# Attention and a feed-forward layer on one core: three copies out of PSUM change engine, one row sum is partly pre-added, and 34 warm-up matmuls are added

## The chip, the cores and the metric

The kernel runs on one core of a Trainium2 chip. Its time is what the device takes for one execution, in microseconds (us). A core has five engines that run side by side and each work through their own instructions in order: TensorE (PE; its weight loads are listed apart as PEld), VectorE (DVE), ScalarE (ACT), GpSimd (POOL) and SyncE (SP, which here only issues DMA transfers). They wait for each other by semaphores. PSUM is the memory into which TensorE writes; VectorE and ScalarE read it, and the large memory beside it is SBUF.

## The reference

For 8 batches of 12 heads, 448 positions and 64 channels:

```python
q_n, k_n = (rmsnorm(q, g_q), rmsnorm(k, g_k))          # x / sqrt(mean(x*x) + 1e-6) * g
scores = scale * np.matmul(q_n, k_n.transpose(0, 1, 3, 2))
attn = softmax(scores)                                  # exp(scores - max) / sum
attn_out = np.matmul(attn, v)
x = attn_out.transpose(0, 2, 1, 3).reshape(3584, 768)
h = x @ w_in                                            # 768 x 2048
out = np.maximum(0.01 * h, h) @ w_out                   # 2048 x 768
```

All inputs and the output are float32.

## The kernel before

The work is cut into `NU` = 24 units. A unit is four heads of one batch, so that three units make a batch. The order of all instructions is written out by hand (`tc.manual_schedule`): what is emitted first on an engine runs first there.

**One unit.** `load` (SP) and `load_v` (POOL) bring q, k and v. `prep_sq` or `prep_sqp` squares (ScalarE or GpSimd), `prep_ssq` sums the squares (VectorE), `prep_rinv` makes the inverse root with Ln and Exp (ScalarE), `prep_norm` multiplies (VectorE), and the result is transposed, in the first units by TensorE (`prep_tr`, `tr`) and from unit 6 on by a DMA (`prep_trd`). `prep_g` then scales the queries with the two gains (VectorE). The scores of a unit come in seven tiles t = 0 to 6, each of 128 x 896 in two PSUM banks (`score`, line 199). `ex` (line 218) makes the exponentials `et` on ScalarE, one instruction per tile, with the bias `eb`. This bias, the negative of a maximum taken from tile 0, comes from `shift_max` and `shift_mm`: a reduce on VectorE (line 236), a small product `dg` (238), two small matmuls (248), a reduce (249) and a scaling (257).

**PSUM.** The score tiles take turns in two tiles of two banks each (`slot`, line 193). The product of the exponentials with v (PV) of the unit before takes one of the two in between (`pv_slot`). The other four banks are handed out by `aux`.

**The end of a unit.** From unit 4 to unit 22 (`narrow`), PV of unit u-1 runs behind the first scores of unit u. `zcol` sums the exponentials with matmuls against ones (line 307, four matmuls of 224 columns for each tile). `pv_out` copies PV from PSUM to SBUF (`x32`, line 319, one buffer), ScalarE takes Ln and Exp of the negative (`zcol_ln`, `zcol_inv`), four DMAs issued by SP spread the inverse sums over the partitions (`rz`, line 334), and `xmul_sb` (VectorE) or `xmul_pool` (GpSimd) multiplies the two (line 344). In units with an entry in `ADDED`, `add_e` first adds that many exponential tiles on VectorE (line 292), so that `zcol` needs fewer matmuls: with 4, it takes 3 tiles and the sum in place of 7 tiles.

**The order in a unit.** Each unit has four steps d = 0 to 3 with score tiles 0; 1 and 2; 3 and 4; 5 and 6. At the start of a unit the order is:

```python
qk(u, STEPS[d]); shift_max(u)
pv_slot(u - 1); zcol(u - 1); shift_mm(u); pv_out(u - 1)
ex(u); zcol_ln(u - 1)
```

Behind each step `fill` puts pieces of the feed-forward layer of earlier batches on TensorE (`moe1`, line 386; `moe2`, line 427; `seven`, line 468), by a fixed cost per piece, and between them small jobs for the other engines: the norms of unit u+2, the inverse sums, differences of weights (`weight_sum`, line 443). VectorE also evicts the results of `moe2` (line 431) and forms sums of activations for `seven` (lines 449 to 458).

**The start.** Units 0 to 2 run before there is any feed-forward work to fill in. There `warm(n, bank)` (line 766) issues n matmuls of 128 x 128 on constant ones; nothing reads their result. Before the change there are groups of 32 and 42 ahead of the first transposes, of 6 ahead of the first `shift_mm`, and of 12, 8, 10, 8 and 12 later, up to 29 us.

Of the kernel before, what the change touches and what calls it, by code (L numbers as in the profile page):

```python
# [18 lines left out]
def kernel(  # L19
# [11 lines left out]
    nc = tc.nc  # L31

    B, H, S, D = q.shape
# [78 lines left out]
    st = {}  # L112
# [25 lines left out]
    def buf(u, name):  # L138
        if name not in st[u]:
            shape, dtype, bufs = SHAPES[name]  # L140
            st[u][name] = prep_p.tile(shape, dtype, tag=name[:2] if bufs == 3 and name != "qkT" else name, bufs=bufs, name=name)
        return st[u][name]
# [3 lines left out]
    def prep_sq(u, c=ALL, tis=BOTH):  # L146
        for ti in tis:
            nc.scalar.activation(buf(u, f"sq{ti}")[:, :, c[0]:c[1]], raw[u][ti][:, :, c[0]:c[1]], AF.Square)  # L148
# [44 lines left out]
    def slot():  # L193
        return psum.tile([P, 2, 512], FP32, tag="sT", bufs=2, name="sT")

    def score(u, t, banks):
        for r in range(2):
            for a in range(2):
                nc.tensor.matmul(banks[a][64 * r:64 * r + 64, 0:S].rearrange("p (t x) -> p t x", t=NS),  # L199
                                 kT(u, r, a, t), qT(u, r, a), start=True, stop=True)  # L200

    def qk(u, steps):
        st[u]["sT"] = []
        for t in steps:
            sT = slot()
            score(u, t, (sT[:, 0], sT[:, 1]))
            st[u]["sT"].append((t, sT))

    def ex(u):
        s = st[u]  # L210
        if "et" not in s:
            s["et"] = epool.tile([P, NS, 2, S], FP16, tag="et", name="et")
        for t, sT in s["sT"]:
            if isinstance(sT, list):
                for a in range(2):
                    nc.scalar.activation(s["et"][:, t, a], sT[a][:, 0:S], AF.Exp, bias=s["eb"], scale=1.0)
            else:
                nc.scalar.activation(s["et"][:, t], sT[:, :, 0:S], AF.Exp, bias=s["eb"], scale=1.0)  # L218
# [62 lines left out]
                                     e[64 * r:64 * r + 64, a], start=(i == 0), stop=(i == len(ets) - 1))  # L281

    HS = S // 2
    ADDED = {u: 4 for u in (10, 11, 13, 16, 17, 19)}
    ADDED.update({3: 5, 4: 5, NU - 1: 5})
    ADDED.update({u: 3 for u in (8, 14, 20, 22)})

    def add_e(u):
        s = st[u]
        s["ea"] = zpool.tile([P, 2, S], FP16, tag="ea", name="ea")  # L290
        for t in range(1, ADDED[u]):
            nc.vector.tensor_tensor(s["ea"], s["et"][:, 0] if t == 1 else s["ea"], s["et"][:, t], op=ALU.add)  # L292

    def z_tiles(u):
        s = st[u]
        ets = [s["et"][:, t] for t in range(NS)]
        return ets[ADDED[u]:] + [s["ea"]] if "ea" in s else ets

# [17 lines left out]
    def pv_out(u):  # L316
        s = st[u]
        s["x32"] = zpool.tile([P, 2, S], FP32, tag="x32", name="x32")
        nc.scalar.copy(s["x32"], s["pslot"][:, :, 0:S])  # L319

    def zcol_ln(u):
        s = st[u]
# [13 lines left out]
    def xmul_sb(u):  # L336
        xmul_pool(u, nc.vector)
# [426 lines left out]
    def warm(n, bank):  # L764
        for x in range(n):
            nc.tensor.matmul(bank[:, P:2 * P], onesp, onesp, start=True, stop=True)

    with tc.manual_schedule():
# [7 lines left out]
        wbank = aux([P, 512], FP32, "warm")  # L776
# [1 line left out]
        for a in range(2):  # L778
            nc.vector.scalar_tensor_tensor(gdup[:, a], grow[:, 0], 0.125, grow[:, 1], op0=ALU.mult, op1=ALU.mult)
        nc.tensor.matmul(gps[:, 0:1], gdup.rearrange("o a d -> o (a d)"), one32, start=True, stop=True)  # L780
        warm(42, wbank)
        prep_sq(0, CA, (0,))
        prep_sq(0, CB, (0,))
        prep_sq(0, ALL, (1,))
# [11 lines left out]
        def tr(u, ti, chunks, tp=None):  # L796
            if tp is None:
                tp = aux([P, NS, P], FP16, "tp")
            for c, copy in chunks:
                for x in range(*c):  # L800
                    nc.tensor.transpose(tp[:, x, :], buf(u, "n16")[:, ti, x].rearrange("p a d -> p (a d)"), ident16)
                copy(buf(u, "qkT")[:, ti, c[0]:c[1]], tp[:, c[0]:c[1]], ti == 0)
            return tp

        tr(0, 0, ((CA, acopy),))
        tr(0, 0, ((CB, acopy),))
        tpk = tr(0, 1, ((K0, vcopy),))
        prep_sq(1, ALL, (0,))
        qk(0, STEPS[0])
        shift_max(0)  # L810
# [7 lines left out]
        load_v(1)  # L818
        load_v(2)
        shift_bank(0)  # L820
        warm(6, st[0]["pb"])
        shift_mm(0)
        prep_ssq(1)

# [56 lines left out]
        for f in range(2):  # L881
            load_w_out(8 * f, 8)
        qk(1, (2,))
        ex(1)
        trn(2, 0, vcopy)
        qk(1, (3,))
# [27 lines left out]
        prep_sqp(5)  # L914
        load_v(5)
        qk(2, (2,))
        ex(2)
        trn(3, 0, vcopy)
        trn(3, 1, vcopy)
# [31 lines left out]
        for u in range(3, NU):  # L951
            for d in range(4):
                if d > 0 or u > 3:
                    qk(u, STEPS[d])
                    if d == 0:
                        shift_max(u)
                        if u == 6:
                            xmul_sb(u - 2)
                        if narrow(u - 1):
                            pv_slot(u - 1)  # L960
                            zcol(u - 1)
                            shift_mm(u)
                            pv_out(u - 1)
                        else:
                            zsum_slot(u - 1)
                            pv(u - 1)
                            shift_mm(u)
                            zinv(u - 1)
                    ex(u)
                    if d == 0 and narrow(u - 1):  # L970
                        zcol_ln(u - 1)
                if d == 2 and ADDED.get(u, 0) > 3 and u < NU - 1:
                    add_e(u)
                    if u > 4:
                        xmul_sb(u - 1)
                jobs = []

                def job(fn, *args):
                    jobs.append(lambda: fn(*args))

                if d == 0:
                    if u == 3:
                        prep_norm(4)
                        gate(4)
                    elif narrow(u - 1):
                        if u < NU - 1:
                            job(zcol_inv, u - 1)
                    else:
                        xmul(u - 1)
                    if u + 4 < NU:  # L990
                        job(load, u + 4)
                    if u + 3 < NU:
                        load_v(u + 3)
                    if u < 6:
                        prep_sqp(u + 3)
                if d == 1 and narrow(u - 1) and not 5 <= u < 8 and ADDED.get(u, 0) < 4:
                    xmul_pool(u - 1)
                if u == NU - 1:
                    if d == 1:
                        job(zcol_inv, u - 1)  # L1000
                if fed(u, d) and u > 3:
                    push(u // NQ - 1)
                if (u, d) in ((3, 1), (4, 0)):
                    for ti in range(2):
                        prep_tr(u + 1, ti, VV)
                if d == 1 and 5 <= u < NU - 1:
                    job(prep_g, u + 1)
                if u + 2 < NU:
                    if d == 1:
                        if ADDED.get(u) == 3:  # L1010
                            job(lambda u: (prep_ssq(u + 2), add_e(u)), u)
                        else:
                            for ti in range(2):
                                job(prep_ssq, u + 2, ALL, (ti,))
                    if d == 2:
                        job(prep_rinv, u + 2)
                        for ti in range(2):
                            job(prep_norm, u + 2, ALL, (ti,))
                        if u > 3:
                            job(prep_trd, u + 2)  # L1020
                if d == 1 and 4 <= u < 8:
                    job(weight_sum, u - 4, 0)
                if d == 0 and 5 <= u < 9:
                    job(weight_sum, u - 5, 1)
                if d == 2 and 6 <= u < 8:
                    job(xmul_sb, u - 1)
                if d == 1 and u == NU - 2:
                    jobs.append(lambda: None)
                    job(add_e, u)
                if u == NU - 2 and d == 0:  # L1030
                    for n, tile_ in ((1, (raws, "rq", 3)), (2, (raws, "rk", 3)), (3, None), (4, (prep_p, "sq", 3))):
                        job(win_sum, n, 1, tile_)
                    for n in (3, 1, 2, 4):
                        job(x_sum, LATE, n)
                if u == NU - 1 and d == 3:
                    job(add_e, u)
                    job(xmul_sb, u - 1)
                if d == 3 and 6 <= u < NU - 3:
                    for ti in range(2):
                        job(prep_sq, u + 3, ALL, (ti,))  # L1040
                fill(u, d, jobs)
# [39 lines left out]
```

## Time and profile before

| | |
|---|---|
| time, median of 4 runs | 418.29 us (417.57 to 418.68) |
| the profiled execution, its own time | 418.64 us |
| its span, from first to last instruction | 416.9 us |
| TensorE busy in 0 to 44 us | 34.15 us |
| TensorE busy in 60 to 121 us | 60.16 us |
| copies of PV on ScalarE (line 319) | 19 of 906 ns |
| warm-up matmuls (line 766) | 130 |

All times inside the execution count from the start of its span. In a timeline row the columns are the start, the duration, the engine, the line of the kernel, the operation with its output and inputs, the shapes, and how many instructions are merged; brackets give the idle time of the engine just before and what ended it. In a row of groups the first figures behind the bar are busy time in all and the mean duration in nanoseconds of one. Matmuls are pipelined and the duration of one (352 ns for 448 columns) is longer than the distance to the next (about 190 ns), so a row of n matmuls is read by the start of the row behind it. Units 5, 6, 7 and 8 start at 69.3, 81.4, 95.5 and 111.2 us.

### The profile page before, as it was taken

The page shows a single profiled execution, that of the slowest core. Times are in us where ns is not written, and L with a number is a line of the kernel's source. Part 1 is how long each engine was busy: PE and PEld are TensorE (multiplying, and loading weights), DVE is VectorE, ACT ScalarE, POOL GpSimd, SP SyncE. Part 2 cuts the span into 40 slices and gives each one's busy share as a digit, 9 for nine tenths or more (in the row PEclk, how much of TensorE's full clock was granted, in tenths as well). Part 3 has the DMA queues.
Part 4 walks back from the last instruction along what each step waited for, and adds up shares of the span by engine and source line. Part 5 has one row for each costly group of instructions (what it writes and reads, how often), then busy time and mean ns, then how long its engine had stood idle before and what let it go on. Part 6 is the DMA issues. An engine that isn't in the chain of part 4 may idle for free.

```text
span 416.9 us, 9315 instructions
## 1 busy us (share of the span) xinstructions
PE 398.8 (96%) x3807; PEld 218.8 (52%) x3807; DVE 301.7 (72%) x485; ACT 303.6 (73%) x474; POOL 68.7 (16%) x70
## 2 busy tenths in 40 slices
PE   7777999999999999999999999999999999999995
PEld 7454444454445544455455544455445557559862
DVE  5888797887688756866668756767669788567762
ACT  5998888778887699867887689867985657644500
POOL 1868432200010200010020200020002202000000
PEclk9999999999999999999999999999999999999999
DMA  5999998889566995678664986688542470023022
GB/s 191 274 257 249 241 249 161 198 156 215 150 155 85 215 246 100 152 179 176 157 156 69 220 205 130 143 183 180 156 91 46 120 165 2 16 68 77 2 75 77
DMA packets 71951, 62.41 MB, mean 150 GB/s; under 512 B 36325, under 2 KB 67045, under 8 KB 71909
## 3 DMA queue, kind: packets, MB, share of 16 engines
q1 hardware_dynamic: 61312, 49.62, 47.5%
q0 software_dynamic: 10272, 11.80, 18.2%
q8 instruction: 30, 0.49, 0.5%
q10 hardware_dynamic: 324, 0.39, 0.3%
q14 instruction: 13, 0.10, 0.1%
HBM read 45.61 MB, written 11.01 MB: 136 GB/s over the span
## 4 chain that ended last, share of the span: by engine, by line
PE 78%; DVE 9%; ACT 8%; issue 2%; DMA 1%; SPq 0%; DVEq 0%; ACTq 0%
PE hps L386 27%; PE sT L199 8%; PE sT L364 5%; PE ma L468 5%; PE md L468 5%; ACT et L218 5%; PE mc L468 5%; PE bank L588 4%; PE bank L468 4%; PE op L427 4%; DVE n L171 3%; PE mb L468 2%; PE zc L307 2%; PE sT L468 2%; DVE sT L236 1%
## 5 line engine op out<-in xcount | busy, mean ns | idle before, releaser
L218 ACT ACTIVATE et<-sT,eb 128x896 f16<-128x896 f32 x166 | 159.5, 1010 | 18.7 <-PE sT L199 16.9
L386 PE MATMUL hps<-xt,win 128*128 128x448 f16 x600 | 120.8, 353 | 0.2 <-DVE xt L373 0.2
L386 PEld LDWEIGHTS <-win 128*128 128x128 f16 x612 | 56.8, 98 | 58.1 <-issue 9.7
L380 ACT ACTIVATE gt<-hps 128x448 f16<-128x448 f32 x100 | 54.0, 556 | 6.1 <-PE hps L386 5.3
L199 PE MATMUL sT<-qkT 64*64 64x448 f16 x664 | 52.4, 363 | 4.4 <-ACT et L218 3.6
L159 DVE TENSOR_REDUCE ssq<-sq 128x14 f32<-128x896 f32 (+2 forms) x49 | 50.1, 1057 | 0.8 <-ACT sq L148 0.7
L468 PEld LDWEIGHTS <-sa 128*128 128x128 f16 x352 | 32.8, 98 | 26.3 <-issue 6.1
L128 POOL DMA_DIRECT2D vt<-in_v_dram x24 | 17.9, 746 | 173.2 <-PE sT L364 166.5
L319 ACT COPY x<-sT 128x896 f32<-128x896 f32 x19 | 17.2, 906 | 34.0 <-DVE sT L249 34.0
L199 PEld LDWEIGHTS <-qkT 64*64 64x64 f16 x672 | 15.4, 104 | 37.8 <-issue 33.4
L468 PEld LDWEIGHTS <-gt 128*128 128x128 f16 x264 | 25.2, 98 | 18.9 <-issue 2.4
L171 DVE TENSOR_TENSOR n<-rq,rinv 128x896 f16<-128x896 f32 (+2 forms) x25 | 28.1, 1125 | 9.5 <-ACT rinv L165 9.5
L344 POOL TENSOR_TENSOR xt<-x,rz 128x896 f16<-128x896 f32 x9 | 19.0, 2114 | 79.3 <-DMA rz<-zs 72.0
L364 PE MATMUL sT<-et,vt 64*64 64x448 f16 x532 | 28.5, 349 | 0.3
L427 PE MATMUL op<-wout,gt 128*128 128x384 f16 x160 | 28.4, 326 | 0.0
L236 DVE TENSOR_REDUCE sT<-sT 128x1 f32<-128x896 f32 x22 | 24.1, 1093 | 4.7 <-PE sT L199 4.5
L292 DVE TENSOR_TENSOR ea<-ea,et 128x896 f16<-128x896 f16 x25 | 15.6, 625 | 15.6 <-ACT et L218 14.8
L364 PEld LDWEIGHTS <-vt 64*64 64x64 f16 x672 | 20.7, 107 | 11.3 <-issue 1.7
L171 DVE TENSOR_TENSOR n<-rk,rinv 128x896 f16<-128x896 f32 (+2 forms) x26 | 26.1, 1010 | 0.0
L427 PEld LDWEIGHTS <-gt 128*128 128x128 f16 x192 | 17.6, 98 | 14.3 <-issue 3.0
L468 PE MATMUL ma<-wout,gt 128*128 128x384 f16 x128 | 23.5, 326 | 0.0
L292 DVE TENSOR_TENSOR ea<-et 128x896 f16<-128x896 f16 x13 | 8.8, 677 | 11.9 <-ACT et L218 11.8
(143 smaller groups left out, 542.5 us busy)
## 6 DMA issues: line engine op xcount, KB each, us to landing
rq<-in_q_dram SPq DMA_DIRECT2D x24, 448.0 KB, 4.4
rk<-in_k_dram SPq DMA_DIRECT2D x24, 448.0 KB, 6.0
out_dram<-ost SPq DMA_DIRECT2D x52, 192.0 KB, 3.1
rz<-zs SPq DMA_DIRECT2D x76, 112.0 KB, 2.3
vt<-in_v_dram POOLq DMA_DIRECT2D x24, 224.0 KB, 5.6
win<-in_moe_w_in_dram POOLq DMA_DIRECT2D x8, 384.0 KB, 13.5
wout<-in_moe_w_out_dram POOLq DMA_DIRECT2D x2, 1536.0 KB, 28.1
out_dram<-ost SPq DMA_DIRECT2D x4, 96.0 KB, 2.1
```

Of the source, the lines that this page charges most:

```text
L159: nc.vector.tensor_reduce(buf(u, "ssq")[:, ti, :, c[0]:c[1]], buf(u, f"sq{ti}")[:, :, c[0]:c[1]], axis=AXL.X, op=ALU.add)
L171: nc.vector.tensor_tensor(buf(u, "n16")[:, ti, c[0]:c[1]].rearrange("p s a d -> p a s d"), src[:, :, c[0]:c[1]], buf(u, "rinv")[:, ti, :, ...
L199: nc.tensor.matmul(banks[a][64 * r:64 * r + 64, 0:S].rearrange("p (t x) -> p t x", t=NS), kT(u, r, a, t), qT(u, r, a), start=True, stop=True)
L218: nc.scalar.activation(s["et"][:, t], sT[:, :, 0:S], AF.Exp, bias=s["eb"], scale=1.0)
L236: nc.vector.tensor_reduce(s["spare"][:, 511:512], sT[:, :, 0:S], axis=AXL.XY, op=ALU.max)
L292: nc.vector.tensor_tensor(s["ea"], s["et"][:, 0] if t == 1 else s["ea"], s["et"][:, t], op=ALU.add)
L344: eng.tensor_tensor(xts[b][:, g], s["x32"], s["rz"], op=ALU.mult)
L364: nc.tensor.matmul(s["pv"][r][64 * a:64 * a + 64, 0:S], vts[u % NV][64 * r:64 * r + 64, a, t], s["et"][64 * r:64 * r + 64, t, a], start=(t ...
L380: nc.scalar.activation(dst, src, AF.Prelu, bias=0.0, scale=1.0, alpha=0.01)
L386: nc.tensor.matmul(hps[:, 0:S], win16[:, kt // 2, kt % 2, ts(ft, P)], xt[:, kt // 2, kt % 2], start=(kt == 0), stop=(kt == KT - 1))
L427: nc.tensor.matmul(op2[:, 0:HC], gt[:, ft, ds(col(t), P)], wout16[:, ft, ds(HC * half, HC)], start=(ft == 0), stop=(ft == FT - 1))
L468: nc.tensor.matmul(bank[:, 0:HC], a[:, f], b[:, f], start=(first and f == 0), stop=(f == HF - 1), skip_group_check=not first)
```

## The change

Four things change:

- `pv_out` of units 4, 5 and 6, which is emitted in units 5, 6 and 7, becomes a copy on VectorE. There it stands behind the bias of the next unit, which is the instruction emitted just before it. The other 16 copies stay on ScalarE.
- Unit 7 gets an entry of 4 in `ADDED`. So VectorE adds its tiles 0 to 3 in step 2 of unit 7, and `zcol` of unit 7 has 16 matmuls instead of 28.
- With this entry, `xmul_sb` of unit 6 follows directly on `add_e`, and the job that made it further behind in the same step is taken out.
- `warm` grows: 48 instead of 42 ahead of the first transposes, 10 instead of 6 ahead of the first `shift_mm`, and new groups of 6 ahead of the first scores of unit 0, of 6 behind tile 2 of unit 1 and of 12 behind tile 2 of unit 2, the last two each ahead of transposes.

On TensorE, VectorE and ScalarE nothing else changes place; the order on SP's and GpSimd's queues is the same.

```diff
-    ADDED = {u: 4 for u in (10, 11, 13, 16, 17, 19)}
+    ADDED = {u: 4 for u in (7, 10, 11, 13, 16, 17, 19)}
...
     def pv_out(u):
         s["x32"] = zpool.tile([P, 2, S], FP32, tag="x32", name="x32")
-        nc.scalar.copy(s["x32"], s["pslot"][:, :, 0:S])
+        if u in (4, 5, 6):
+            nc.vector.tensor_copy(s["x32"], s["pslot"][:, :, 0:S])
+        else:
+            nc.scalar.copy(s["x32"], s["pslot"][:, :, 0:S])
...
-        warm(42, wbank)
+        warm(48, wbank)
...
         tpk = tr(0, 1, ((K0, vcopy),))
+        warm(6, wbank)
...
-        warm(6, st[0]["pb"])
+        warm(10, st[0]["pb"])
...
         qk(1, (2,))
+        warm(6, st[1]["pb"])
         ex(1)
...
         qk(2, (2,))
+        warm(12, st[2]["pb"])
         ex(2)
...
-                if d == 2 and 6 <= u < 8:
+                if d == 2 and u == 6:
                     job(xmul_sb, u - 1)
```

## The prediction

> **What bounds the kernel now.** I read the page's busy shares and its chain of waits first, then the busy time stage by stage, then the timeline around each edit.
>
> ```profile
> PE 398.8 (96%) x3807; PEld 218.8 (52%) x3807; DVE 301.7 (72%) x485; ACT 303.6 (73%) x474; POOL 68.7 (16%) x70
> ...
> PE 78%; DVE 9%; ACT 8%; issue 2%; DMA 1%; SPq 0%; DVEq 0%; ACTq 0%
> ```
>
> TensorE is busy for 96% of the span and holds 78% of the chain that ended last; ScalarE and VectorE have a quarter of their time free. The next view is the busy time of each engine by stretch (microseconds, PE, PEld, DVE, ACT, POOL, granted clock, DMA share):
>
> ```profile
> 0.00:44.00 44.00, 34.15 (x460) 22.77 (x461) 33.63 (x66) 36.25 (x55) 26.09 (x36) 1.00 0.99 244
> ...
> 60.00:121.00 61.00, 60.16 (x572) 29.53 (x570) 46.78 (x67) 49.08 (x77) 8.33 (x8) 1.00 0.81 173
> ```
>
> The start-up, to 44 us, is a chain through VectorE and ScalarE: PE idles 9.85 us there. From 60 to 121 us, where units 5 to 8 run, PE idles 0.84 us. So time taken off ScalarE is worth only the PE gaps that it causes. The timeline (start, duration, engine, line) shows the worst place, the start of unit 6:
>
> ```profile
> 85.09 0.91 ACT L319 COPY x<-sT 128x896 f32<-128x896 f32 x1 [4.46 <-DVE sT L249]
> 85.09 0.16 DVE L257 TENSOR_SCALAR eb<-sT 128x1 f32<-128x1 f32 x1
> 85.89 1.01 ACT L218 ACTIVATE et<-sT,eb 128x896 f16<-128x896 f32 x1
> ...
> 86.64 0.69 PE L199 MATMUL sT<-qkT 64*64 64x448 f16 x8
> ...
> 87.18 0.39 ACT L329 ACTIVATE zs<-zs 128x224 f32<-128x224 f32 x1
> ...
> 87.48 3.69 ACT L218 ACTIVATE et<-sT,eb 128x896 f16<-128x896 f32 x4
> ...
> 88.67 0.38 PE L199 MATMUL sT<-qkT 64*64 64x448 f16 x4
> 89.42 0.38 PE L199 MATMUL sT<-qkT 64*64 64x448 f16 x4 [0.36 <-ACT et L218]
> ```
>
> The bias was ready at 85.25, but the first exponential started at 85.89, behind the copy. The eight score matmuls at 86.64 took 0.69 us where others take 0.57, and the last four of the next eight waited until 89.42 for the exponential that frees their tile.
>
> **The change, part by part.** The profiled execution is 418.64 us (span 416.9 and 1.74 around it); the median of the four times is 418.29, which is 0.35 lower. I sum against 418.64 and then take off 0.35.
>
> *The three copies, off ScalarE.* Each frees 0.906 us of ScalarE ahead of an exponential, but the exponential can start only when the bias is there, so it moves 0.6 us.
> - Unit 5: exp 0 moves from 72.76 to 72.15. The next pair of scores starts on PE at 74.12 and exp 1 at 74.56, 0.44 later, the same distance as at 92.44 to 92.88 where ScalarE is marked as waiting for PE. PE sets exp 1 already: gain 0. The 0.30 us that PE loses inside the scores at 76.03 (0.87 instead of 0.57) stays.
> - Unit 6: exp 0 runs 85.29 to 86.30, so the scores at 86.64 lose no 0.12. The two small ScalarE operations end near 87.0 instead of 87.57, and exp 1 starts at 86.64 + 0.44 = 87.08 instead of 87.48. Exp 2 starts 0.89 later (the spacing of the four in 3.69 us) and ends at 88.98 instead of 89.38. The scores that waited until 89.42 start at 89.02: gain 0.40. From there PE runs on without a visible gap, so the 0.40 reaches the end.
> - Unit 7: exp 1 started 0.55 after its scores, behind a ScalarE prelu, but PE shows no gap from 92 to 118 us: gain 0.
> Bounds: 0 (another wait holds the same matmuls) to 0.70 (the gap of unit 5 closes too). I take 0.40, since both rows name what ended the wait.
>
> *The three copies, on VectorE.* No row shows this copy there. These rows are near (groups: count, busy, mean ns):
>
> ```profile
> L236 DVE TENSOR_REDUCE sT<-sT 128x1 f32<-128x896 f32 x22 | 24.1, 1093 | 4.7 <-PE sT L199 4.5 <-ACT sq L148 0.2
> ...
> L292 DVE TENSOR_TENSOR ea<-et 128x896 f16<-128x896 f16 x13 | 8.8, 677 | 11.9 <-ACT et L218 11.8
> ...
> L636 DVE COPY v<-bank 128x448 f32<-128x448 f32 x5 | 3.1, 620 | 0.7 <-PE bank L588 0.6
> ```
>
> The reduce reads the same shape from PSUM in 1.09 us; two half-size copies take 1.24. The top bound is 1.9: the weight difference at L443 takes 1.66 instead of 0.95 while POOL works. I take 1.09, the same elements in one instruction. The bias stays ahead of it. It ends at 73.2, 86.3 and 99.8, and the second score tile of each pair now waits for it; PE gets there at 74.3, 86.8 and 101.7. Cost 0; without that cover it is a PE stall of up to 0.3 us at unit 6 (1.9 us for the copy). Behind it in VectorE's queue: in units 5 and 6 an eviction that waits for PE anyway (idle 2.11 and 1.50 us before it); in unit 7 a weight difference, the scaling of unit 8's queries, two sums of squares and a second difference, all done by 102.75, now 103.85. Their users are the scores at 111.25 and the Ln at 107.11.
>
> *Unit 7's row sum.* VectorE adds four exponential tiles (0.68 + 2 x 0.63 = 1.93 us), and the product of unit 6 (1.08 us, VectorE) moves from behind the second running sum to a place ahead of unit 9's normalisation. VectorE had 4.98 us idle before 107.73. The third addition waits for exp 3, at 105.9, then 106.6, then the product to 107.66: just inside. The product's four broadcast DMAs were first issued at 101.31 and become usable 4.4 us later (117.08 to 121.56 in unit 8), before 106.6. SP's and POOL's queues keep their order. Cost 0; without the cover (0 to 3.0 us) the normalisation is late, and its transposed result is needed only in unit 9, near 127.8.
>
> TensorE drops 12 of 28 matmuls in unit 7's column sum:
>
> ```profile
> 112.88 0.85 PE L307 MATMUL zc<-et,onesr 128*32 128x224 f16 x28
> ...
> 113.33 0.29 DVE L238 TENSOR_TENSOR dg<-ident,sT 128x128 f16<-128x128 f16 x1
> ...
> 113.67 0.23 PE L248 MATMUL sT<-dg,onesp 128*128 128x64 f16 x2
> ```
>
> 28 matmuls take 0.79 us to the next matmul, 20 take 0.60 (129.47 to 130.07) and 16 take 0.50 (160.02 to 160.52): 0.29 less. But that next matmul needs dg, ready at 113.62. The reduce before dg started at 112.21 only because the moved product stood at 110.54 in VectorE's queue. Without it the reduce can start 0.44 after its scores at 111.25, and dg is ready at 113.1, before PE's 113.38. Gain 0.29 (bounds 0 and 0.29).
>
> *34 more warm-up matmuls.*
>
> ```profile
> 1.16 3.60 PE L766 MATMUL warm<-onesp 128*128 128x128 f16 x32 [1.16 <-DVE onesp L80]
> ...
> 5.20 2.91 PE L766 MATMUL warm<-onesp 128*128 128x128 f16 x42
> ...
> 8.31 0.90 PE L801 MATMUL tp<-ident,n 128*128 128x128 f16 x8 [0.21 <-DVE n L171]
> ```
>
> The first 32 take 3.52 us to the next instruction, 110 ns each; the 12 at 12.43 take (0.84 - 0.22)/11 = 56 ns. The 42 start (2.91 - 0.22)/41 = 66 ns apart on the mean: about eight of them slow (41 x 10 / 54), to near 6.0 us, the rest fast. Six more add 0.34, and PE had 0.36 between the slot after the 42nd (7.95) and the first transposes. I take 0.05 loss; bounds 0 and 0.66 (all six at 110 ns, no slack). This is on the path: transposes, ScalarE's copies (ending 9.91), the first scores at 9.98. The other four groups stand in PE waits: 6 in the 0.94 us before 9.98, 4 in the 0.98 before 11.97, 6 in the 0.70 before 24.61, 12 in the 1.33 before 34.06; even at 110 ns each (0.66, 0.44, 0.66, 1.32) they fit. Cost 0. Gain 0 too: no matmul after 8 us is slow (the transposes' maximum is 230 ns, their median 219), so nothing is there to warm.
>
> The Trainium skill (TensorE: Matmul & The Clock Gate, Part 1) says that the full clock is granted after a busy window of about 3.4 us that runs free of the kernel's start. Here PE is slow from 1.16 to near 6.0, longer than one such window and shorter than two, which fits; no run here shows the moment moving. By that rule the switch could fall up to about 8.0 us, the six would then cost the full 0.34 in many executions, and my estimate for the sum would be about 0.2 us worse.
>
> **Sum.** -0.40 - 0.29 + 0.05 = -0.64: 418.00 for that execution, 417.65 for the median.
>
> **Rivals.**
> 1. *More than forecast: unit 5's gap closes too.* For: 0.30 us are lost at 76.03. Against: the 0.44 us from scores to exp. -0.94: 417.35.
> 2. *Hidden anyway at unit 6.* For: the copy on VectorE frees the second tile only at 86.3, and a 1.9 us copy would end at 87.15. Against: at 1.09 it is 0.5 us early. -0.24: 418.05.
> 3. *The first transposes late.* For: only 0.02 us of slack are left. Against: this profile has it. -0.69 + 0.66: 418.26.
> 4. *Slower: the moved product blocks VectorE.* If its broadcast lands late, unit 9's normalisation, two microseconds of sums and the reduce of unit 8 are late behind it and PE waits at 113.4. VectorE has 0.6 us of slack there, so a wait past 107.2 costs one for one, and past 107.9 the kernel is slower than before. For: the product stands 3.9 us earlier than before. Against: the longest of eight landings on POOL is 5.94 us after the first issue (306.85 to 312.79), which is 107.25. At 8 us it would be 109.3: -0.64 + 2.1 = +1.46, 419.75.
> That the copy still holds the exponential is excluded by the order on VectorE: reduce, bias, copy.
>
> **How the numbers follow.** Chances: forecast 0.52, rival 1 0.17, rival 2 0.13, rival 3 0.11, rival 4 0.07. Two tenths of a per cent (0.84 us) is about what a measurement of this kernel can tell from no change; the four times spread over 1.1 us. The forecast is 0.2 us short of that bound, so three in ten of its chance count as faster; of rival 1 most; a little of rivals 2 and 3 and all of 4 count as slower: 0.32, 0.55, 0.13. The range reaches from below rival 1 (416.9, with 0.4 for the median) to above rival 3 (418.6).
>
> **What would show it.** Right: exp 0 within 0.05 us of the bias in units 5 to 7; a VectorE copy of 1.05 to 1.25 us; the second scores of unit 6 with a wait of 0.25 instead of 0.5; sixteen column-sum matmuls and no idle before the pair of unit 8; the first transposes at 8.3. Wrong: a wait of PE for VectorE at those scores, an idle of VectorE before the product of unit 6, transposes after 8.6, or slow matmuls after 10 us in before that this execution lacks.

## The result, and the profile after

The kernel takes 417.00 us after the change (median of 38 executions, 416.64 to 418.85) against 418.25 before (58 executions). The ratio is 0.9973, with a 95% interval of 0.9966 to 0.9979: 1.1 us or 0.27% faster (0.9 to 1.4 us). The prediction had 417.65, and 416.9 to 418.6 as its range. The profiled execution took 417.13 us, with a span of 415.3.

The page of the kernel after, busy times and chain of waits:

```profile
PE 400.4 (96%) x3829; PEld 220.3 (53%) x3829; DVE 305.7 (74%) x491; ACT 301.5 (73%) x471; POOL 68.7 (17%) x70
...
PE 83%; ACT 8%; DVE 7%; issue 1%; DVEq 0%; ACTq 0%
```

TensorE still bounds it. It is busy 1.6 us longer, with the added warm-ups, in a span 1.5 us shorter, and it holds 83% of the chain instead of 78%; VectorE's share fell from 9% to 7%.

The timeline of the kernel after, unit 6 and the start of unit 7 (start, duration, engine, line; lines from 320 on stand three higher than before):

```profile
85.16 0.16 DVE L257 TENSOR_SCALAR eb<-sT 128x1 f32<-128x1 f32 x1
85.24 1.08 DVE L320 COPY x<-sT 128x896 f32<-128x896 f32 x1
85.42 1.01 ACT L218 ACTIVATE et<-sT,eb 128x896 f16<-128x896 f32 x1 [4.71 <-DVE eb L257]
...
86.72 0.57 PE L199 MATMUL sT<-qkT 64*64 64x448 f16 x8
...
89.43 2.77 PE L430 MATMUL op<-wout,gt 128*128 128x384 f16 x16
...
93.86 1.08 DVE L347 TENSOR_TENSOR xt<-x,rz 128x896 f16<-128x896 f32 x1
93.95 1.58 PE L389 MATMUL hps<-xt,win 128*128 128x448 f16 x6
...
95.46 0.38 PE L199 MATMUL sT<-qkT 64*64 64x448 f16 x4
```

The first exponential is 0.47 us earlier, the scores at 86.72 take 0.57 us instead of 0.69, and the output matmuls behind the next scores start at 89.43, where the kernel before had them at 89.73. Unit 6 began 0.08 us later in this execution, so 0.38 us is gained up to here. But the six matmuls at 93.95 now take 1.58 us, where they took 1.30 before (94.25): they read the product `xt`, which VectorE makes from 93.86 to 94.94. Unit 7's scores start at 95.46; before, at 95.48.

The same view for the row sum of unit 7, in unit 8:

```profile
105.91 0.63 DVE L292 TENSOR_TENSOR ea<-ea,et 128x896 f16<-128x896 f16 x1 [0.93 <-ACT et L218]
106.45 1.08 DVE L347 TENSOR_TENSOR xt<-x,rz 128x896 f16<-128x896 f32 x1
...
107.71 1.09 DVE L171 TENSOR_TENSOR n<-rq,rinv 128x896 f16<-128x896 f32 x1 [0.17 <-ACT rinv L165]
...
112.86 0.47 PE L307 MATMUL zc<-et,onesr 128*32 128x224 f16 x12
112.86 0.29 DVE L238 TENSOR_TENSOR dg<-ident,sT 128x128 f16<-128x128 f16 x1
113.16 0.27 PE L307 MATMUL zc<-ea,onesr 128*32 128x224 f16 x4
...
113.36 0.23 PE L248 MATMUL sT<-dg,onesp 128*128 128x64 f16 x2
```

Sixteen matmuls stand where 28 stood, dg is ready at 113.15, and the pair of small matmuls of line 248 follows at 113.36 (before: 113.67) with no idle. Every unit from 5 on has such a pair, and below its start is the mark by which TensorE's progress is compared between runs. These 0.3 us are kept: from unit 8 to unit 20 the pair of line 248 is 0.31 us earlier in every unit. Then, between the pairs of units 20 and 21, another 0.55 us appears that no part of the change touches. The timeline before, at that place, where unit 19's broadcast and product are made in unit 20:

```profile
306.85 2.48 SPq L334 DMA_DIRECT2D rz<-zs  x4
...
312.79 2.29 POOL L344 TENSOR_TENSOR xt<-x,rz 128x896 f16<-128x896 f32 x1 [8.74 <-DMA rz<-zs]
313.05 2.97 DVE L171 TENSOR_TENSOR n<-rq,rinv 128x896 f16<-128x896 f32 x1
...
320.40 0.22 PE L248 MATMUL sT<-dg,onesp 128*128 128x64 f16 x2 [0.49 <-DVE dg L238]
```

and after:

```profile
306.55 2.48 SPq L337 DMA_DIRECT2D rz<-zs  x4
...
310.90 2.20 POOL L347 TENSOR_TENSOR xt<-x,rz 128x896 f16<-128x896 f32 x1 [7.15 <-DMA rz<-zs]
...
312.08 1.30 DVE L458 TENSOR_TENSOR sa<-gt 128x512 f16<-128x512 f16 x1
...
313.64 1.08 DVE L171 TENSOR_TENSOR n<-rq,rinv 128x896 f16<-128x896 f32 x1
...
319.54 0.23 PE L248 MATMUL sT<-dg,onesp 128*128 128x64 f16 x2
```

Before, GpSimd's product of unit 19 starts 5.94 us after the first issue of the four broadcast DMAs; after, 4.35 us. A two-input operation that VectorE starts while GpSimd's product runs is held until the product ends: the normalisation of 1.08 us takes 2.97 before, a running sum of 0.42 takes 1.30 after. With the late product VectorE loses 1.9 us instead of 0.9, reaches dg late, and TensorE waits 0.49 us. Where the 1.6 us of the product's delay come from is the main question of the experiments.

Another 0.75 us, by which the two profiled executions differ, stand behind the last matmul, and they belong to this one execution of the kernel before. VectorE's last operation, behind which the last store goes out, starts 4.93 us before the end of the span (416.86):

```profile
411.93 0.56 DVE L475 TENSOR_TENSOR ost<-bank,ost 128x384 f32<-128x384 f32 x1 [0.74 <-PE bank L468]
```

In a second profile of the same kernel (e10 below) it is 4.19 us (to 415.92), and in the twelve others 4.17 to 4.20:

```profile
411.73 0.56 DVE L475 TENSOR_TENSOR ost<-bank,ost 128x384 f32<-128x384 f32 x1 [0.74 <-PE bank L468]
```

In the first of the two the store's packets run on to 415.17, and a packet of 16 KB of the queue that the experiments are about starts among them, at 413.16. How many executions of the kernel before end in this way isn't known.

### The profile page after: what moved, and what is told of

It is laid out like the page before. It is cut to its first block, busy times and chain, and to the rows that moved or that the text cites. A ratio compares the mean times of both kernels' runs of the same rounds, so it can differ in the third digit from the quotient of the medians.

```text
span 415.3 us, 9366 instructions
## 1 busy us (share of the span) xinstructions
PE 400.4 (96%) x3829; PEld 220.3 (53%) x3829; DVE 305.7 (74%) x491; ACT 301.5 (73%) x471; POOL 68.7 (17%) x70
## 4 chain that ended last, share of the span: by engine, by line
PE 83%; ACT 8%; DVE 7%; issue 1%; DVEq 0%; ACTq 0%
PE hps L389 27%; PE sT L199 8%; PE sT L367 5%; PE ma L471 5%; PE md L471 5%; PE mc L471 5%; PE op L430 5%; ACT et L218 4%; PE bank L591 4%; PE bank L471 4%; PE mb L471 3%; PE zc L307 2%; PE warm L769 2%; PE sT L471 2%; DVE n L171 2%
## 5 line engine op out<-in xcount | busy, mean ns | idle before, releaser
L322 ACT COPY x<-sT 128x896 f32<-128x896 f32 x16 | 14.5, 907 | 25.5 <-DVE sT L249 25.5
L171 DVE TENSOR_TENSOR n<-rq,rinv 128x896 f16<-128x896 f32 (+2 forms) x25 | 26.2, 1051 | 4.5 <-ACT rinv L165 4.5
L292 DVE TENSOR_TENSOR ea<-ea,et 128x896 f16<-128x896 f16 x27 | 16.9, 625 | 16.7 <-ACT et L218 15.7
```

The costliest lines, as they stand in the source:

```text
L171: nc.vector.tensor_tensor(buf(u, "n16")[:, ti, c[0]:c[1]].rearrange("p s a d -> p a s d"), src[:, :, c[0]:c[1]], buf(u, "rinv")[:, ti, :, ...
```

## The experiments

The prediction's three edits were run one by one. In the expectations, quoted as they were written, the broadcast and product near 307 to 315 us are called unit 18's and the pair near 320 us unit 19's; by the right count they are unit 19's and unit 21's. After them came a theory for the place at 310 us, called F: the packets of the DMA queue named "q8 instruction" (30 of 16 KB, 0.49 MB, on both pages) are TensorE's own code. Its 3807 matmuls and 3807 weight loads make 7614 instructions, 254 for each packet; in each of the fourteen traces TensorE starts 252 to 254 instructions per packet between the first and the last. By the theory the place of each packet depends on how many instructions TensorE had before it, and one that falls into a broadcast makes it late (a collision, below). The rival is that the place is chance, or that the row sum gains there by itself.

All runs (the median of n executions; the ratio to the kernel before, run on the same chip; the time of GpSimd's product of unit 19 from the first issue of its broadcast; TensorE's idle before the pair of unit 21; the number of TensorE's instructions):

| run | median, n | ratio, interval | product after issue | PE idle | instructions |
|---|---|---|---|---|---|
| before | 418.25, 58 | | 5.94 | 0.49 | 7614 |
| after | 417.00, 38 | 0.9973, 0.9966 to 0.9979 | 4.35 | 0 | 7658 |
| e1_warm_only | 418.36, 12 | 1.0007, 0.9994 to 1.0020 | 4.37 | 0 | 7682 |
| e2_sum_only | 417.02, 9 | 0.9973, 0.9963 to 0.9982 | 4.37 | 0 | 7590 |
| e3_copies_only | 418.07, 12 | 1.0000, 0.9992 to 1.0009 | 5.56 | 0.49 | 7614 |
| e4_no_warm | 417.30, 11 | 0.9975, 0.9966 to 0.9985 | 4.36 | 0 | 7590 |
| e5_minus12 | 417.65, 12 | 0.9993, 0.9985 to 1.0001 | 4.37 | 0 | 7590 |
| e6_sum_plus12 | 418.43, 11 | 1.0007, 0.9998 to 1.0015 | 5.63 | 0.49 | 7614 |
| e7_product_first | 416.77, 5 | 0.9968, 0.9956 to 0.9980 | 4.35 | 0 | 7658 |
| e8_front42 | 416.92, 11 | 0.9986, 0.9967 to 1.0005 | 4.35 | 0 | 7658 |
| e9_sum_plus12_again | 417.93, 10 | 0.9996, 0.9983 to 1.0009 | 5.54 | 0.49 | 7614 |
| e10_before_again | 417.69, 1 | | 5.65 | 0.49 | 7614 |
| e11_after_again | 417.21, 12 | 0.9979, 0.9970 to 0.9989 | 4.38 | 0 | 7658 |
| e12_product_first_again | 416.58, 6 | 0.9960, 0.9946 to 0.9973 | 4.35 | 0 | 7658 |

The last column is twice the count of TensorE's matmuls on the page. Every profile with 7614 shows the late product and the idle, five executions of three kernels; none of the nine others does at this place.

### The three edits alone

e1_warm_only, the 34 warm-ups alone:

```diff
-        warm(42, wbank)
+        warm(48, wbank)
...
         tpk = tr(0, 1, ((K0, vcopy),))
+        warm(6, wbank)
...
-        warm(6, st[0]["pb"])
+        warm(10, st[0]["pb"])
...
         qk(1, (2,))
+        warm(6, st[1]["pb"])
...
         qk(2, (2,))
+        warm(12, st[2]["pb"])
```

> The kernel before with the 34 added warm-up matmuls and nothing else. Theory A (the forecast's steps, corrected by the traces: the matmuls ahead of the first transposes can only delay them, and everything else about them is hidden): 0 to +0.35 us against the kernel before; first scores at 10.0 to 10.3 us. Theory B (the part of the gain that the forecast misses comes from the start: more matmuls keep PE's clock up, or the start more even): -0.4 to -0.9 us, and slow matmuls in some executions of the kernel before.

No gain: 418.36. The place at 310 us is clean in its profile, but the same thing is found in unit 9:

```profile
133.49 2.69 SPq L334 DMA_DIRECT2D rz<-zs  x4
...
139.89 2.07 POOL L344 TENSOR_TENSOR xt<-x,rz 128x896 f16<-128x896 f32 x1 [9.06 <-DMA rz<-zs]
140.44 2.48 DVE L171 TENSOR_TENSOR n<-rq,rinv 128x896 f16<-128x896 f32 x1 [0.32 <-ACT rinv L165]
...
143.44 1.46 PE L468 MATMUL md<-tw,gt 128*128 128x384 f16 x8 [0.70 <-DVE ost L475]
```

The product comes 6.40 us after the first issue, the normalisation takes 2.48 us, and TensorE falls 0.86 us behind between the pairs of units 9 and 10. An instruction packet lies at 137 us in this profile, inside that broadcast. So the warm-ups alone move the trouble rather than remove it.

e2_sum_only, the row sum and the moved product alone:

```diff
-    ADDED = {u: 4 for u in (10, 11, 13, 16, 17, 19)}
+    ADDED = {u: 4 for u in (7, 10, 11, 13, 16, 17, 19)}
...
-                if d == 2 and 6 <= u < 8:
+                if d == 2 and u == 6:
```

> The kernel before with unit 7's pre-added row sum and the moved product of unit 6 and nothing else. Theory A: -0.29 us, the twelve matmuls, with the pair of small matmuls of unit 8 at 113.4 instead of 113.7. Theory B says the same. A third theory, that moving the product out of the way of unit 8's first reduce is worth more than the matmuls, would give -0.5 or more.

417.02, the whole measured gain. Up to the last matmul its trace has 0.28 us at unit 8 and 0.55 us between the pairs of units 20 and 21, and nothing else.

e3_copies_only, the copies of units 4 to 6 on VectorE alone:

```diff
-        nc.scalar.copy(s["x32"], s["pslot"][:, :, 0:S])
+        if u in (4, 5, 6):
+            nc.vector.tensor_copy(s["x32"], s["pslot"][:, :, 0:S])
+        else:
+            nc.scalar.copy(s["x32"], s["pslot"][:, :, 0:S])
```

> The kernel before with the three copies on VectorE and nothing else. Theory A: unit 6 gains 0.38 us at its second and third pair of scores and gives 0.28 back at the feed-forward matmuls behind (93.9 us), which then wait for the product of unit 5 on VectorE: -0.1 us. Rival: the copies shift the broadcasts and the stores into a better order later on: -0.5 us or more.

418.07 and a ratio of 1.0000: no change that can be measured. In its trace TensorE gains 0.11 us from the pair of unit 6 to that of unit 7; the rest of the 0.4 us is given back at the product, as in the kernel after.

e4_no_warm, the change without the 34 warm-ups (the diffs of e2 and e3 together):

> The changed kernel without the 34 added warm-up matmuls (copies and row sum only). Theory A: -0.4 us against the kernel before, and up to 0.35 us faster than the changed kernel. Theory B: clearly slower than the changed kernel, by 0.4 to 0.9 us.

417.30 against 417.00 for the whole change. Both profiles are clean at 310 us, so this pair shows the warm-ups without that loss, though not with an equal number of instructions: up to 0.3 us by the medians, in the direction opposite to the forecast, though the two ratios (0.9975 and 0.9973) don't tell them apart. What the warm-ups do is plainer in the granted clock of the executions. A mean clock of 0.998 or more has 39 of 92 executions of the kernel before, 6 of 11 here, and 44 of 50 of the changed kernel; the others have 0.990 to 0.996. Among the executions of before, the median is 418.01 us in the first class, 418.41 with 0.993 or less. The 44 of the changed kernel have a median of 417.02, so 1.0 us of the change is there between executions that all had the full clock.

### Theory F: twelve hidden matmuls less, twelve more

e5_minus12, the kernel before without the twelve warm-ups in the wait near 12.4 us:

```diff
-        warm(12, wb)
```

> The kernel before without the twelve warm-up matmuls that stand in PE's wait near 12.4 us. No other instruction changes, and the twelve are hidden in that wait (they end at 13.27 in the profile before). Theory F (the transfer of 16 KB on the instruction queue, which in the profile before falls at 310.0 us into unit 18's broadcast of 306.85 to 311.6, comes after a fixed number of PE's instructions and makes that broadcast late): with 12 matmuls, 24 rows of PE, fewer ahead of it the transfer comes later, after the broadcast; GpSimd's product of unit 18 ends under 5.0 us after the first DMA issue (before 5.94), VectorE's norm after it takes 1.08 us instead of 2.97, PE has no idle before the pair of unit 19 (before 0.49), and the time is 0.45 to 0.6 us less than before. Rival (the place of the transfer has nothing to do with PE's instruction count, or the event is the execution's chance): the event stays in the profile, or is missing without the time moving: within 0.15 us of before.

417.65 against 418.23 of the kernel before on this chip, 0.58 us less; the ratio of 0.9993 (to 1.0001) is weaker than the medians. The trace is plainer: from unit 5 to unit 20 this kernel stands 0.08 to 0.09 us behind the one before, and from unit 21 on 0.45 to 0.47 ahead of it. The loss of 0.55 us is gone, and nothing else moved up to the last matmul. The packets show why. Each of these answers covers one microsecond of the DMA queues; the row GB/s has 40 slices of 25 ns. The kernel before, 310 to 311 and then 311 to 312 us:

```profile
GB/s 179 108 179 179 143 251 251 108 251 179 143 179 179 179 251 143 799 215 215 72 215 215 72 108 73 36 72 0 0 0 0 0 0 0 0 0 0 0 0 0
...
q8 instruction: 1, 0.02, 5.5%
...
GB/s 0 0 0 0 0 0 0 0 0 0 36 0 0 0 36 0 0 0 0 36 0 0 36 0 0 36 0 0 0 36 0 0 0 36 0 0 0 36 0 0
DMA packets 8, 0.01 MB, mean 7 GB/s; under 512 B 0, under 2 KB 8, under 8 KB 8
```

The same for e5_minus12, 310 to 311 us:

```profile
GB/s 108 108 36 251 143 36 215 251 108 287 179 179 179 143 251 179 179 215 215 179 251 143 143 287 108 179 215 36 108 0 36 656 0 0 0 0 0 0 0 0
...
q8 instruction: 1, 0.02, 7.2%
```

and for the kernel after, 310 to 311 us:

```profile
GB/s 323 143 143 287 143 215 251 72 215 251 72 108 36 36 36 0 0 0 0 0 0 0 0 0 0 0 0 0 0 0 0 0 0 0 0 0 0 0 0 0
```

The slice with 799 or 656 GB/s is the instruction packet (5.5% of 16 engines for 1 us, so 0.9 us of one engine). Before, it falls at 310.40, with the broadcast under way. Most of the broadcast is done at 310.7, but single packets of about 1 KB follow one by one to 311.95. That is how a share of the broadcast looks that is held on one DMA engine behind the large packet. In e5 the packet falls at 310.78, behind the last piece, and after 311 there is no packet at all; in the kernel after it falls at 304.3, ahead of the broadcast. That the stragglers are on the packet's own engine isn't in the rows; that they come with it is.

The other broadcasts say the same. The fourteen traces hold 266 of them (19 each, 512 packets of 896 bytes in each). In 43 an instruction packet starts 0.2 to 3.6 us after the first issue: there the last piece of the broadcast is through 4.15 to 5.57 us after the issue, 4.58 in the median. In the other 223 it is through after 3.81 to 4.38 us, 3.89 in the median, and only three of these take more than 4.2. Being late isn't yet a loss: TensorE falls back behind seven of the 43 (unit 19 in five profiles, one in e1, one in e11), and not behind the others.

How far a number of instructions moves a packet isn't constant: 24 less move it 0.2 us (e2) and 0.4 us (e5) later, 44 more some 6 us earlier, where 18 instructions per microsecond (7614 in 417 us) would give 1.3 and 2.4 us. Counted from the first issue of the broadcast, the packet comes after 3.15 to 3.55 us in the five profiles with 7614 instructions and after 3.72 to 3.85 in the three with 7590, where the broadcast is nearly through: less than 0.2 us separate a late product from a punctual one. What starts the transfer was not found.

e6_sum_plus12, the edit of e2 with twelve warm-ups in the wait of 1.33 us near 34 us, and e9_sum_plus12_again, the same kernel once more:

```diff
         load_v(5)
         qk(2, (2,))
+        warm(12, st[2]["pb"])
         ex(2)
```

> The row-sum edit alone with twelve extra warm-up matmuls in PE's wait of 1.33 us near 34 us, so that PE's instruction count from unit 8 on is that of before again. Theory F: the transfer near 310 us falls into unit 18's broadcast again; GpSimd's product ends over 5.3 us after the first issue, an operation of VectorE near 312 takes 2 to 3 us, PE idles some 0.5 us near 320; only the matmuls' 0.29 us remain of the gain, so 0.3 to 0.5 us under before and about 0.55 slower than the row-sum edit alone (417.02). Rival (the row sum gains on VectorE or ScalarE by itself): 1.1 to 1.25 us under before, as the row-sum edit alone.

> The row-sum edit with the twelve hidden warm-up matmuls once more, for another execution's profile: its median was 418.43, 1.4 above the row-sum edit alone, where the one late broadcast at unit 18 shows only 0.55 us. Theory F alone (one collision): the collision at unit 18 is there again and is all that PE loses against the row-sum edit alone (0.49 to 0.6 us), apart from the start-up. Rival (the shifted transfers also meet other broadcasts): a second operation of VectorE near a product of GpSimd takes 2 us or more in some other unit, with a second PE idle of 0.4 to 0.9 us. Median 418.0 to 418.5 in both.

Both profiles have the late product (5.63 and 5.54 us), a VectorE operation of 2.3 us and the idle of 0.49 us: twelve matmuls in a wait at 34 us bring back a loss at 320 us. Against the kernel before, both gain 0.28 to 0.29 us at unit 8 and nothing from there to the last matmul (within 0.02 us), so only the matmuls' part is left, as F says. The time fell further back than F says: 418.43 and 417.93, a median of 418.26 for the 21, or 1.2 us above e2 instead of 0.55. The rival of e9, a second collision, isn't in either profile. What e9's profile has is a late load in the start-up:

```profile
32.80 1.52 PE L364 MATMUL pv<-et,vt 64*64 64x448 f16 x28 [1.85 <-DMA vt<-in_v_dram]
```

With it this execution loses 1.1 us between its first scores and 44 us that e6's does not; e6's, at 417.18, is the shortest of its 11 executions. Only 4 of the 21 have a mean clock of 0.998 or more, against 5 of 9 of e2. So the start-up holds the rest at least in part; how often each of these happens can't be told from one profile each, and that part stays open. The 0.75 us at the end of the first profile are no help here: neither e6's nor e9's profile has them.

e10_before_again, the kernel before once more:

> The kernel before once more, for another execution's profile. Theory F: the transfer on the instruction queue stays within 1 us of 310.0 and the product of unit 18 ends over 5.3 us after the first issue again, with a VectorE operation of 2 us or more and a PE idle near 0.5 us ahead of the pair of unit 19; where the execution is one of those under 417.7 us, the collision is missing. Rival (the collision was that one execution's chance): the product ends 4.4 us after the first issue and PE has no idle there, at a time near 418.2.

```profile
306.65 2.49 SPq L334 DMA_DIRECT2D rz<-zs  x4
...
312.30 2.24 POOL L344 TENSOR_TENSOR xt<-x,rz 128x896 f16<-128x896 f32 x1 [8.45 <-ACT et L218]
312.52 2.30 DVE L458 TENSOR_TENSOR sa<-gt,sa 128x512 f16<-128x512 f16 x1
...
320.21 0.22 PE L248 MATMUL sT<-dg,onesp 128*128 128x64 f16 x2 [0.49 <-DVE dg L238]
```

The late product was no chance: it is there in this execution too, with the packet at 309.8, and VectorE is held at another instruction, a running sum of 0.41 us that takes 2.30. One detail of the expectation fell: at 417.69 the execution is one of the short ones and has the collision nevertheless, so the spread of the kernel before isn't this. The two profiles of this kernel differ by 0.95 us in time: 0.2 us in the start-up and the 0.75 us behind the last matmul.

e11_after_again, the changed kernel once more:

> The changed kernel again, on the chip of the next run. Theory F: no collision at unit 18 in this execution either (the transfer near 304, the product 4.3 to 4.5 us after the first issue, no PE idle ahead of the pair of unit 19), the gap of 0.28 us at 93.95 is there; most executions show a mean clock of 0.998 or more. 416.8 to 417.2. Rival (the missing collision was that execution's luck): a late product at unit 18 as in the kernel before.

417.21, the product 4.38 us after the issue, no idle, the packet at 304, and the 1.58 us of the matmuls at the product of unit 5 again. F holds. A smaller collision is in this trace, too: a packet meets the broadcast of unit 10, which is through 5.38 us after its issue, and TensorE loses 0.13 us ahead of the pair of unit 12.

### What the change leaves behind

e7_product_first and e12_product_first_again, the changed kernel with the product of unit 5 ahead of the normalisation of unit 8:

```diff
                     if d == 2:
                         job(prep_rinv, u + 2)
+                        if u == 6:
+                            job(xmul_sb, u - 1)
                         for ti in range(2):
                             job(prep_norm, u + 2, ALL, (ti,))
...
-                if d == 2 and u == 6:
-                    job(xmul_sb, u - 1)
```

> The changed kernel with VectorE's product of unit 5 ahead of unit 8's normalisation in unit 6's second step; PE's instructions are the same. If the gain at unit 6 is given back at 93.95 only because the product stands behind the normalisation (product 93.86 to 94.94, matmuls 1.58 us instead of 1.30), the product comes 1 to 2 us earlier, the matmuls at 93.95 take 1.2 to 1.3 us without a gap, and unit 7's scores start 0.28 us earlier: 0.25 to 0.3 us faster than the changed kernel, 416.7. Rival (something else is late there, or the delayed normalisation makes unit 8's transposes late): no gain, or up to 0.5 us slower.

> The changed kernel with the product of unit 5 ahead of unit 8's normalisation, again beside the changed kernel itself. If the gap at 93.95 is the only thing that the copies leave behind, 0.2 to 0.3 us faster than the changed kernel on the same chip (about 416.7), with no gap at 93.6 and none new up to unit 9. Rival: within 0.1 us of the changed kernel.

e7's timeline:

```profile
91.50 1.08 DVE L347 TENSOR_TENSOR xt<-x,rz 128x896 f16<-128x896 f32 x1
92.50 1.09 DVE L171 TENSOR_TENSOR n<-rq,rinv 128x896 f16<-128x896 f32 x1
...
93.59 1.30 PE L389 MATMUL hps<-xt,win 128*128 128x448 f16 x6
94.82 0.38 PE L199 MATMUL sT<-qkT 64*64 64x448 f16 x4
```

The product comes 2.0 us earlier against the matmuls, these take 1.30 us again, and in both executions TensorE gains 0.39 us from unit 6 to unit 7 against the kernel before, where the changed kernel gains 0.11. Beside the changed kernel on the same chip it takes 416.58 against 417.21; over both runs 416.61 (11 executions) against 417.08 (50). This is the fastest kernel of the study, 1.7 us faster than the one before (ratio 0.9960, 0.9946 to 0.9973). The 0.28 us are shown by the traces; the other 0.2 of the medians is within their spread.

e8_front42, the changed kernel with 42 warm-ups in front and six more near 34 us, so that the number of instructions from there on is the same:

```diff
-        warm(48, wbank)
+        warm(42, wbank)
...
-        warm(12, st[2]["pb"])
+        warm(18, st[2]["pb"])
```

> The changed kernel with 42 warm-up matmuls in the first group again instead of 48, and 18 instead of 12 in the wait near 34 us, so that PE's instruction count is the same from there on. If the six hold the first transposes, as the profile of the changed kernel shows (matmuls to 8.60, VectorE's normalised keys at 7.25 with 1.08 us behind it), the transposes start up to 0.34 us earlier and the kernel is 0.1 to 0.34 us faster than the changed one. Rival (the load of the keys sets the transposes in most executions, or the clock is full later): 0 within 0.1, or slower by up to 0.2.

416.92 (416.62 at best; the changed kernel 416.64 at best): the rival, no difference that shows. The start of the changed kernel explains why both answers occur:

```profile
5.20 3.40 PE L769 MATMUL warm<-onesp 128*128 128x128 f16 x48
...
8.44 0.61 PE L804 MATMUL tp<-ident,n 128*128 128x128 f16 x8
```

Here the 48 end at 8.60 and the transposes start behind them, at 8.44, without a wait. In e12 the 48 take 2.85 us from 4.92 and the transposes wait 0.34 us for VectorE at 8.12. The first group is slow for a part of its length that differs between executions, and only where that is long do the six cost anything.

## Why the prediction was right, and where it was not

The time is in the range and the direction was right, but the 0.65 us missing from the forecast (417.65 against 417.00) and one of its two gains were of another kind than it said. Rival 1, which comes nearest to the measured time (417.35), isn't what happened either: unit 5's scores still take 0.87 us (at 76.10). That the time came out faster than the forecast, and not slower, is owed to a term that the prediction lacks.

**The copies, on ScalarE.** Unit 6 went as forecast up to the output matmuls (0.38 us gained for 0.40), unit 5 and unit 7 gained 0 as forecast: exp 1 of unit 5 waits for TensorE. The first exponential followed the bias by 0.10 us, not 0.05. The step that failed is "From there PE runs on without a visible gap, so the 0.40 reaches the end". The matmuls at 94.25 had no gap before because VectorE's product, from 93.78 to 94.86 there, was just in time for those that read it:

```profile
93.78 1.08 DVE L344 TENSOR_TENSOR xt<-x,rz 128x896 f16<-128x896 f32 x1
...
94.25 1.30 PE L386 MATMUL hps<-xt,win 128*128 128x448 f16 x6
```

For matmuls 0.38 us earlier it was not, and 0.28 were given back. The net is 0.11 us (e3: ratio 1.0000). With the product moved, e7 has 0.39 of the forecast 0.40. The rows before the change would have shown it: VectorE works without a pause from 86.75 to 95.3 us and ends nothing earlier because an exponential is earlier.

**The copies, on VectorE.** Right: 1.08 us each for 1.09, behind the bias, and the evictions behind them waited for TensorE anyway.

**The row sum.** Right in every step: the third addition at 105.91, the product to 107.53, the normalisation at 107.71 with the wait it had before, dg ready at 113.15 (forecast 113.1), 0.28 us for 0.29. Of the slower rival, the product waiting for its broadcast, nothing was seen at unit 8. Two readings beside it were off without effect: 117.08 to 121.56 are 4.5 us, not 4.4, and the page has nine such products on GpSimd, not eight.

**The warm-ups.** The cost of 0.05 was mis-sized for the profiled execution. Its keys were ready 0.33 us earlier than in the profile before, but its first scores came 0.09 later, so the six cost about 0.4 us there; at the median they cost nothing that e8 could show. "Gain 0 too: no matmul after 8 us is slow" was read off one execution whose clock was full. Others lose it. The busy time by stretch in e5, which lacks twelve warm-ups near 12 us (us, busy of PE, PEld, DVE, ACT, POOL, granted clock, DMA):

```profile
10.00:12.00 2.00, 1.23 (x21) 0.86 (x18) 1.47 (x3) 1.90 (x3) 0.51 (x1) 0.65 0.96 315
12.00:14.00 2.00, 0.89 (x8) 0.13 (x3) 1.97 (x4) 1.67 (x5) 1.47 (x1) 0.50 1.00 371
14.00:16.00 2.00, 2.00 (x21) 1.40 (x18) 2.00 (x4) 1.97 (x4) 2.00 (x4) 0.50 1.18 280
16.00:20.00 4.00, 3.93 (x47) 2.39 (x44) 2.83 (x7) 3.75 (x5) 4.00 (x7) 0.82 1.06 197
```

The shares of the clock make 6.8 us at half speed, from about 10.6 to 17.4, and this execution loses 0.42 us from its first scores (0.35 earlier than before) to 44 us (0.07 later). Half the clock isn't always paid for: e6's profile has 3.4 us of it and loses 0.04 us over the same stretch. None of e5's 12 executions had a mean clock of 0.998; of the changed kernel's, 44 of 50 had. So the kernels with the added warm-ups have a full clock more often, worth at most 0.3 us in the medians by e4; that the clock is what these 0.3 us are isn't shown.

**What the prediction lacks.** The largest part of the gain, 0.55 us, is the collision at 310 us, which no step or rival named. The row sum removed it by taking 24 instructions out of TensorE's code (e2), in e5 twelve removed matmuls did the same, and with the count restored it was back (e6, e9); the 266 broadcasts show the packet's part in it. The trace before showed all of it: a product 5.94 us after its issue where the others on GpSimd take 4.3 to 4.7 (the prediction used this very row as a bound), a normalisation of 2.97 us, and an idle of 0.49 us on TensorE that VectorE ended. The Trainium skill (Runtime: NRT & Kernel Launch, Instruction fetch mechanics) says that an engine's code is refilled in blocks of 16 KiB or 256 instructions through a DMA queue of its own, at a cost that is mostly hidden. The 254 instructions per packet agree, and TensorE itself shows no wait at the packet of 310.40; the cost is on the data transfers beside it, which the section doesn't speak of.

The sum by what was found: 0.28 (matmuls), 0.11 (copies), 0.55 (collision) are 0.94 us. TensorE gives 0.09 of them back near 358 us, in unit 23, in the traces that have both the copies and the row sum; the cause is open. So 0.85 us are shown up to the last matmul, where 1.0 is measured among executions with a full clock, 1.1 by the ratio and 1.25 by the medians. What fills the difference stays open; up to 0.3 of the clock and the drawn-out last store, seen in one profile of the two of before, are candidates. For the profiled pair alone the account closes: 0.94 less 0.09, less 0.08 in the start-up, and 0.75 behind the last matmul are 1.52 of 1.51 us (418.64 to 417.13). Without the collision and the clock the gain would have been 0.3 to 0.4 us, where 0.64 was forecast.

## What to carry to other kernels

A gap closed on the busiest engine counts only up to the next place where another engine was just in time: look ahead along that engine's rows, up to the length of the gain, for work that ends just as it is needed. And before a change is costed, look in the profile for transfers and operations that take longer than their like; an edit anywhere that changes the number of instructions can move them, so compare such variants with the number held equal.

## What the runs showed of the hardware

- Adding or removing twelve matmuls that are hidden in a wait near the start moved TensorE's work behind 320 us by 0.55 us, through a 16 KB packet that comes 275 to 300 us later.
- VectorE's operations with two inputs from SBUF that start during GpSimd's product of 2.2 us wait for its end: 0.41 us became 2.30, 1.08 became 2.97. In the fourteen traces there are 47 of them, and they end 0.28 us (running sums of 0.42) or 0.95 us (normalisations of 1.08) behind the product, whenever they start. A copy from PSUM at 311.61 in the kernel after, during the same product, kept its 0.56; so did additions with one input from PSUM (0.56) and reductions of one input (1.08). The Trainium skill (SBUF — State Buffer, SBUF: two separate sides) says that GpSimd and VectorE share a port there, which agrees with these rows.
- TensorE's clock fell to half near 11 us in some executions, for 6.8 us in e5's and 3.4 us in e6's profile; the time at which the first warm-ups turn fast differs between executions (48 of them took 3.40 us in one, 2.85 in another). The prediction drew on the Trainium skill (TensorE: Matmul & The Clock Gate, Part 1) for a window that runs free of the kernel's start, and for a busy window of about 3.4 us, and said that no run showed the moment moving. These do, and the two lengths are one and two such windows.
